# Forming the first network's operand for both groups of heads in one step, with the second group's heads placed pairwise the other way round

## The chip, the core and the metric

The kernel runs on one core of a Trainium2 chip. The metric is device time in microseconds (us) of one execution; lower is better. The time before is the median of three runs.

## What is computed

Landmark attention for 4 batches of 8 heads (576 rows, head size 64, 32 landmarks), followed by two feed-forward networks over the 2304 rows:

```python
q_lm = q.reshape(B, H, m, S // m, D).mean(axis=3)     # 32 landmarks a head
k_lm = k.reshape(B, H, m, S // m, D).mean(axis=3)
A = sm(q, k_lm); Bm = sm(q_lm, k_lm); C = sm(q_lm, k)
Z = Bm.transpose(0, 1, 3, 2) / (norms of Bm)
for _ in range(6):
    Z = 2 * Z - Z @ Bm @ Z
attn = A @ Z @ C @ v
h = attn @ w_in;  x = leaky_relu(h) @ w_out           # first network, 512 -> 2048 -> 512
xn = x / rms(x) * rms_g                               # second network
out = (silu(xn @ w_gate) * (xn @ w_val)) @ w_out2
```

## The kernel before

The kernel never forms the attention's output. For each batch `b` it computes W = Z C v (64 x 32 a head, `wt`) and multiplies it into `w_in` before anything meets A: for each quarter `c` of the 2048 columns, M = W^T w_in, a 32 x 512 block for each head. A and M, each split into a high and a low part of the type fp32r, then feed the first network's hidden layer: h = A M, summed over all heads. M is the "operand of the first network" in the title.

**Heads and groups.** The eight heads are two groups `g` of four (NG = 2). A group's four heads lie side by side in tiles of 128 partitions: the generator `heads` gives for head `h` the 64 input rows it uses (0 to 63 for even `h`, 64 to 127 for odd) and its 32 landmark partitions, `32 * h` to `32 * h + 32`. So a product of a head of 64 input rows and 32 output rows uses a 64x32 part of TensorE's 128x128 array: its rows are given by where the inputs lie, its columns by the output's partitions. In both groups head 0 stands on rows 0 to 63 and columns 0 to 31, head 1 on rows 64 to 127 and columns 32 to 63, head 2 on rows 0 to 63 and columns 64 to 95, head 3 on rows 64 to 127 and columns 96 to 127. Half of the array's eight 64x32 parts are used by one group, and the other group uses the same half.

**Where such sets of four products stand.** `form_m` (line 740): M, 64x32 parts, 512 columns of output, for each of 4 batches, 4 quarters and 2 groups, so 32 sets. `chain` (line 512: landmark scores, 304 columns, two sets for each batch and group; later smaller ones at lines 578, 616, 632, 659) and `soft_a` (line 682: scores of A, 288 columns, two sets for each batch and group). All of these are plain fp32, and the trace shows each such product as two MATMUL instructions, so a set of four products is eight instructions. The large products (lines 773 and 839: the first network; 1120 and 1363: the second) are fp32r, one instruction each, on the whole array.

**Evacuation of M.** A set of `form_m` writes one bank of PSUM (tag `pa`, two banks in all, shared by `chain` and `soft_a`). A copy to the high part follows (ScalarE or VectorE, helper lines 335 and 337), then a subtraction on VectorE for the low part (line 750). Then the bank is free.

**Order.** All instructions are put in order by a planner in the kernel (`Order`). A task is a Python generator that yields the engines it could use with an assumed length, and what it needs: events, or free buffers of a ring, as `("pa", 1)`. The planner picks among the tasks that can run the one with the lowest start and due time; the due time of a task is its deadline less a length from the table `PAR`. The order it finds is the program's; on the chip each engine runs its own list and waits by semaphores.

```python
def form_m(b, c, g):                       # before: one group at a time
    ...
    yield pe4(512), [("pa", 1), f"chain{b},{g}"] + before
    ...
    e = yield act(450) + dve(512), []
    copy(e, hi, pm)
    yield dve(512), []
    nc.vector.tensor_sub(lo, pm, hi.bitcast(F32))      # line 750
    order.free(pm)
```

Of the kernel before, what the change touches and what calls it, by code (L numbers as in the profile page):

```python
# [8 lines left out]
F32 = mybir.dt.float32  # L9
# [21 lines left out]
    "unit": 2400,  # L31
    "chain": [18400, 20600, 27900, 75000],
    "soft": 5000,
    "form": 2600,
    "conv": 600,
    "load": 400,
    "raw": 6600,
# [130 lines left out]
def pe4(n, count=1):  # L168
    return [("pe", int(count * (n / 0.6 + 26)))]
# [35 lines left out]
def landmark_attention_then_two_ffns(  # L205
# [272 lines left out]

    def heads():

        for h in range(4):
            a = 64 * (h % 2)
            yield h, h // 2, slice(a, a + 64), slice(32 * h, 32 * h + 32)

    def chain(b, g):

# [19 lines left out]
        for i in range(2):  # L508
            yield pe4(HB), [(pa, 1)]
            sc = bank(pa)  # L510
            for h, p, rows, lm in heads():
                nc.tensor.matmul(
                    sc[lm, :HB], qsum[rows, p], kt[p][rows, i * HB:(i + 1) * HB],
                    start=True, stop=True,
                )
            on = yield act(HB - 30) + dve(HB), []
            copy(on, e[:, i * HB:(i + 1) * HB], sc[:, :HB])
            order.free(sc)
# [55 lines left out]

        yield pe4(P, 4), [(pa, 1)]
        pr = bank(pa)
        for h, p, rows, lm in heads():
            nc.tensor.matmul(
                pr[lm, :M], bb[lm, 1, :], bb[lm, 1, :], start=True, stop=True
            )  # L580
# [31 lines left out]
        def cv(out, c):  # L612
            vt = v_in[b, g]
            n = P if c < NKC - 1 else KREST
            for h in range(4):
                nc.tensor.matmul(
                    out[32 * h:32 * h + 32, :],
                    et[:n, c * P + 32 * h:c * P + 32 * h + 32],
                    vt[:n, c, 64 * h:64 * h + 64],
                    start=(c == 0), stop=(c == NKC - 1),  # L620
                )

        for k in range(NEWTON):
            last = k == NEWTON - 1
            n0 = 1 if last else 0
            needs = [(pa, 1)]
            if k == 1:
                needs += [f"v{b},{g}", f"turned{b},{g},0", f"turned{b},{g},1"]
            yield pe4((320, 320, 128)[min(k, 2)]), needs
            pr = bank(pa)  # L630
            for h, p, rows, lm in heads():
                nc.tensor.matmul(
                    pr[lm, :2 * M].rearrange("p (a m) -> p a m", m=M)[:, n0:],
                    rz[lm, 0, :], rz[lm, 2 * n0::2, :], start=True, stop=True,
                )
            if k == 0:
                nc.tensor.transpose(pr[:, 2 * P:3 * P], e[:, 3 * P:4 * P], ident)
                nc.tensor.transpose(pr[:KREST, 3 * P:], e[:, 4 * P:S], ident)
            elif k == 1:
                for c in range(NKC):  # L640
                    cv(pr[:, 2 * P:2 * P + 64], c)
                order.free(v_in[b, g])
            yield dve(2 * M), []
            nc.vector.tensor_add(
                rz[:, 2 * n0::2, :],
                pr[:, :2 * M].rearrange("p (a m) -> p a m", m=M)[:, n0:],
                rz[:, 1 + n0:, :],
            )
            if k == 0:
                order.aside(turned(1, pr))  # L650
            elif k == 1:
                order.aside(scaled(pr))
            else:
                order.free(pr)
        yield pe4(64), [(pa, 2), ("wt", 1), f"cv{b},{g}"]
        pw = bank(pa), bank(pa)
        wt = new("wt", wq, [P, 2, M])
        for h, p, rows, lm in heads():
            nc.tensor.matmul(
                pw[p][rows, :M], t1[lm, :], z[lm, :], start=True, stop=True  # L660
            )
# [10 lines left out]
    def soft_a(b, g, h):  # L672

        j = 2 * b + h
        before = [f"soft{j - 1},{i}" for i in range(NG)] if j else []
        before += [f"soft{j},0"] if g else []
        yield pe4(SB), [("pa", 1), ("x2", 1), f"ksum{b},{g}", f"q{b},{g}"] + before
        kt, qt = k_in[b, g], q_in[b, g]
        nb = SB // M
        ps = bank("pa")  # L680
        for _, p, rows, lm in heads():
            nc.tensor.matmul(
                ps[lm, :SB], kt[p][rows, S:], qt[p][rows, h * SB:(h + 1) * SB],
                start=True, stop=True,
            )
        if h == 1:
            order.free(kt[0], qt[0])
        x2 = new("x2", att, [P, 2 * SB])
        order.begun(f"soft{j},{g}")
        yield dve(SB), []  # L690
        xf, xt = x2[:, :SB], x2[:, SB:]
        x = xf.rearrange("p (a m) -> p a m", m=M)
        st = att_tile([P, 2, nb], "st")
        nc.vector.transpose(xf, ps[:, :SB])  # L694
        order.free(ps)
        yield dve(SB), []
        nc.vector.reduce_max(st[:, 0, :], x, axis=AX.X)
        e = yield pool(SB - 60) + dvep(SB), []
        engine[e].tensor_sub(x, x, st[:, 0, :].unsqueeze(2).to_broadcast([P, nb, M]))
        yield act(SB), []  # L700
        nc.scalar.activation(xf, xf, AF.Exp, scale=SCALE / GRP)
        yield dve(SB), []
        nc.vector.reduce_sum(st[:, 0, :], x, axis=AX.X)
        yield dvep(nb), []
        nc.vector.tensor_scalar_add(st[:, 0, :], st[:, 0, :], EPS_SM)
        yield dvep(nb + 30), []
        nc.vector.reciprocal(st[:, 1, :], st[:, 0, :])
        e = yield pool(SB - 60) + dvep(SB), []
        engine[e].tensor_mul(x, x, st[:, 1, :].unsqueeze(2).to_broadcast([P, nb, M]))
        yield dve(SB), []  # L710
        nc.vector.transpose(xt, xf)
        e = yield act(SB) + dve2(SB), [f"at{j}"] if g else [("at_hi", 1)]
        if g == 0:
            at_hi[j], at_lo[j] = part("at_hi", at_all, SB)
            order.begun(f"at{j}")
        copy(e, at_hi[j][:, g, :], xt)
        e = yield pool(SB) + dvep(SB), []
        engine[e].tensor_sub(at_lo[j][:, g, :], xt, at_hi[j][:, g, :].bitcast(F32))
        order.free(x2)
        order.done(f"a{j},{g}")  # L720

    m_order = list(dict.fromkeys((j // 2, f // q4) for _, j, f in units))
    m_left = {(b, g): NC for b in range(B) for g in range(NG)}
    mm_hi, mm_lo = {}, {}

    def form_m(b, c, g):
        first = g == 0
        before = [f"mm{b},{c}"] if g else [("m_hi", 1)]
        i = m_order.index((b, c))
        if first and i:  # L730
            before.append("mm{},{}".format(*m_order[i - 1]))
        before += [f"w_in{c},{2 * g + p}" for p in range(2)]
        yield pe4(512), [("pa", 1), f"chain{b},{g}"] + before
        if first:
            mm_hi[b, c], mm_lo[b, c] = part("m_hi", m_all, 512)
            order.begun(f"mm{b},{c}")
        hi, lo = mm_hi[b, c][:, g, :], mm_lo[b, c][:, g, :]
        pm = bank("pa")
        for h, p, rows, lm in heads():
            nc.tensor.matmul(  # L740
                pm[lm, :], wt_in[b, g][rows, p], w_in_sb[c][rows, 2 * g + p, :].bitcast(F32),
                start=True, stop=True,
            )
        m_left[b, g] -= 1
        if m_left[b, g] == 0:
            order.free(wt_in[b, g])
        e = yield act(450) + dve(512), []
        copy(e, hi, pm)
        yield dve(512), []
        nc.vector.tensor_sub(lo, pm, hi.bitcast(F32))  # L750
        order.free(pm)
        order.done(f"m{b},{c},{g}")
# [682 lines left out]
    with tc.manual_schedule():  # L1435
# [60 lines left out]
        for b in range(B):  # L1496
            when = first(lambda j, f: j == 2 * b)
            for g in range(NG):
                before = PAR["chain"][b] + PAR["load"] - g * 200 + PAR["form"]
                order.add(when, before, load_k(b, g))  # L1500
                order.add(when, before - PAR["q"], load_q(b, g))
                order.add(when, before - PAR["v"][b], load_v(b, g))
                order.add(when, PAR["chain"][b] + PAR["form"], chain(b, g))
                for h in range(2):
                    w = first(lambda j, f: j == 2 * b + h)
                    order.add(w, PAR["soft"] + PAR["last"] * (b == B - 1), soft_a(b, g, h))
                for c in range(NC):
                    w = first(lambda j, f: (j // 2, f // q4) == (b, c))
                    order.add(w, PAR["form"] + PAR["last"] * (b == B - 1), form_m(b, c, g))
        nc.sync.dma_start(g_sb, rms_g)  # L1510
        order.add(due(0), PAR["h"], ffn1_h(0))
        order.add(due(0) + 1500, PAR["y"], ffn1_y(0))
# [90 lines left out]
```

## Time and profile before

| | |
|---|---|
| median of 3 runs | 855.62 us (853.45 to 857.05) |
| profiled execution: its own time, and the span from its first to its last instruction | 853.5 us, 851.4 us |
| busy share of the span: TensorE (PE), VectorE (DVE), ScalarE (ACT), GpSimd (POOL) | 96%, 74%, 40%, 17% |
| mean granted TensorE clock | 0.984 of full speed |
| line 740 (M): instructions, busy time | 256, 33.5 us, between 36.7 and 345.2 us |

The profile is of one execution. PE is matrix multiplication, PEld the loading of weights beside it. A line number is that of the kernel before. A row of a timeline gives start and length in us, engine, line, operation, what is written and read, shape, and the number of instructions that were merged; in brackets the idle time of the engine before it, and what ended it. A merged row's length runs to the end of its last instruction, which lies past the start of the next row because matmuls are pipelined; what a row costs PE is read from its start to the start of the next row.

### The profile page before, as it was taken

What the parts mean: (1) busy time and instruction counts of PE and PEld (TensorE: products, weight loads), DVE (VectorE), ACT (ScalarE), POOL (GpSimd) and SP (SyncE); (2) the same over time, 40 slices, a digit from 0 to 9 for tenths busy, and PEclk for the clock granted to TensorE, in tenths of its full rate; (3) what the DMA queues carried; (4) which work ended last, traced back from release to release, by engine and by line L of the source; (5) the groups of instructions that cost most, each with busy time, mean ns of one, the idle gap of its engine ahead of it and who ended that gap; (6) DMA issues with size and microseconds to landing.
All of it is one profiled execution on the core that took longest, in us unless ns stands there. A gap on an engine that the chain in (4) does not pass through costs nothing. (4 is left out here: it accounts for less than half of the span.)

```text
span 851.4 us, 17835 instructions
## 1 busy us (share of the span) xinstructions
PE 821.6 (96%) x6902; PEld 754.5 (89%) x6902; DVE 631.2 (74%) x1405; ACT 340.8 (40%) x816; POOL 147.2 (17%) x183
## 2 busy tenths in 40 slices
PE   4899999999999999999989999999999999999998
PEld 1388789988888887999979999999999999999998
DVE  6699885556465866778679877777777659998991
ACT  4677474444344544545444343333333222222220
POOL 2241231002040531210032131211222000000000
PEclk9599999999999999999999999999999999999999
DMA  9874773453723703546421243222321399653601
GB/s 326 315 252 138 246 258 121 167 181 113 247 79 111 252 30 107 163 161 195 167 85 56 68 131 106 106 105 106 106 92 57 118 349 356 188 169 111 182 31 50
DMA packets 80549, 131.97 MB, mean 155 GB/s; under 512 B 6224, under 2 KB 50256, under 8 KB 79568
## 3 DMA queue, kind: packets, MB, share of 16 engines
q1 hardware_dynamic: 80464, 130.84, 46.0%
q8 instruction: 54, 0.88, 0.4%
q14 instruction: 31, 0.25, 0.1%
HBM read 87.95 MB, written 42.86 MB: 154 GB/s over the span
## 5 line engine op out<-in xcount | busy, mean ns | idle before, releaser
L839 PE MATMUL py<-g_hi,w 128*128 128x288 f32 x1024 | 210.7, 299 | 0.0
L839 PEld LDWEIGHTS py<-g_hi,w 128*128 128x128 f32 x1024 | 163.5, 188 | 12.0 <-issue 11.2
L839 PE MATMUL py<-g_lo,w 128*128 128x288 f32 x512 | 150.7, 294 | 0.0
L773 PE MATMUL ph<-at,mm 128*128 128x288 f32 x768 | 127.5, 305 | 1.5 <-ACT hs L792 1.4
L773 PEld LDWEIGHTS ph<-at,mm 128*128 128x128 f32 x768 | 109.5, 191 | 16.7 <-ACT hs L792 6.0
L789 ACT ACTIVATE g_hi<-ph 128x288 fp32r<-128x288 f32 x128 | 52.5, 410 | 127.1 <-PE ph L773 114.0
L839 PEld LDWEIGHTS py<-g_lo,w 128*128 128x128 f32 x512 | 96.3, 188 | 0.0
L795 DVE TENSOR_TENSOR g_lo<-hs,g_hi 128x288 fp32r<-128x288 f32 x104 | 49.2, 473 | 55.3 <-ACT hs L792 54.8
L792 ACT ACTIVATE hs<-ph 128x288 f32<-128x288 f32 x128 | 52.1, 407 | 0.0
L1214 ACT ACTIVATE cc<-cc 128x288 f32<-128x288 f32 x48 | 21.4, 445 | 68.4 <-DVE cc L1211 68.2
L1185 ACT ACTIVATE hs<-ph 128x288 f32<-128x288 f32 x48 | 19.6, 408 | 62.3 <-PE ph L1120 62.3
L1120 PE MATMUL py<-w,wt 128*128 128x288 f32 x288 | 43.2, 298 | 0.0
L1120 PE MATMUL py<-w,mm 128*128 128x288 f32 x288 | 42.6, 296 | 0.3 <-DVE g_lo L1178 0.3
L373 ACT ACTIVATE raw<-raw 128x512 f32<-128x512 f32 x52 | 35.2, 680 | 16.5 <-DMA raw<-w_val 10.2
L335 ACT COPY hs<-ph 128x288 f32<-128x288 f32 (+1 forms) x49 | 18.8, 384 | 57.0 <-PE ph L1363 33.0
L1120 PEld LDWEIGHTS py<-w,wt 128*128 128x128 f32 x288 | 39.9, 189 | 0.5 <-DVE g_lo L1181 0.2
L1120 PEld LDWEIGHTS py<-w,mm 128*128 128x128 f32 x288 | 39.6, 188 | 0.8 <-DVE g_lo L1178 0.5
L1188 DVE TENSOR_TENSOR cc<-g_hi,py 128x288 f32<-128x288 f32 x48 | 21.6, 450 | 23.8 <-PE py L1120 23.8
L740 PE MATMUL pa<-w_in,wt 64*32 64x512 f32 x256 | 33.5, 626 | 2.3 <-DVE x L694 1.3
L795 POOL TENSOR_TENSOR g_lo<-hs,g_hi 128x288 fp32r<-128x288 f32 x24 | 20.9, 872 | 66.7 <-ACT hs L792 64.5
L1196 DVE TENSOR_TENSOR us<-cc,g_lo 128x288 f32<-128x288 f32 x46 | 22.9, 498 | 12.2 <-ACT cc L1214 12.2
L1196 DVE TENSOR_TENSOR us<-hs,cc 128x288 f32<-128x288 f32 x45 | 26.9, 599 | 5.6 <-DMA u_dram<-us 1.7
(302 smaller groups left out, 1743.1 us busy)
## 6 DMA issues: line engine op xcount, KB each, us to landing
u_dram<-us SPq DMA_DIRECT2D x48, 288.0 KB, 2.1
wo_dram<-ct SPq DMA_DIRECT2D x42, 256.0 KB, 2.3
raw<-w_out SPq DMA_DIRECT2D x20, 512.0 KB, 4.3
y_dram<-ys SPq DMA_DIRECT2D x60, 144.0 KB, 2.2
yin<-y_dram SPq DMA_DIRECT2D x14, 576.0 KB, 4.8
yin<-u_dram SPq DMA_DIRECT2D x20, 384.0 KB, 6.2
raw<-w_gate SPq DMA_DIRECT2D x12, 512.0 KB, 3.7
raw<-w_val SPq DMA_DIRECT2D x12, 512.0 KB, 4.8
```

The source lines that it names most:

```text
L373: nc.scalar.activation(high.bitcast(F32), high.bitcast(F32), AF.Prelu, scale=2.0 ** -112, alpha=2.0 ** 32)
L740: nc.tensor.matmul(pm[lm, :], wt_in[b, g][rows, p], w_in_sb[c][rows, 2 * g + p, :].bitcast(F32), start=True, stop=True,)
L773: nc.tensor.matmul(ph[:, :SB], w[b, c][:, g, o:o + P], x[j][:, g, :], start=(n == 0), stop=(n == 3 * NG - 1),)
L789: nc.scalar.activation(g_hi[u], ph[:, :SB], AF.Prelu, alpha=0.01)
L792: nc.scalar.activation(hs, ph[:, :SB], AF.Prelu, alpha=0.01)
L795: engine[e].tensor_sub(g_lo[u], hs, g_hi[u].bitcast(F32))
L839: nc.tensor.matmul(yacc[i][d][:, :SB], w[f][:, d * P:(d + 1) * P], x[u], start=(f == f0 and n == 0), stop=(f == f1 - 1 and n == 2),)
L1120: nc.tensor.matmul(pp[:, :SB], w[f][:, i, c * P:(c + 1) * P], x[b][1][:, k, c, :], start=(first and n == 0), stop=(n == 5), skip_group_che ...
L1185: nc.scalar.activation(sg, pp["a"][:, :SB], AF.Silu)
L1188: nc.vector.tensor_add(f32("c21", "cc"), t["u2"], pp["c"][:, :SB])
L1196: engine[e].tensor_mul(us[0][:, h, :], sg, t[name])
L1214: nc.scalar.activation(t["c12"], t["c12"], AF.Silu)
```

## The change

`form_m` is one task for both groups: it asks for two banks of `pa`, for the chains of both groups and for all four pieces of `w_in`, issues the eight products of the two groups one behind the other, and then starts two tasks `split_m`, one for each group, that evacuate as before. In `heads`, the landmark partitions of head `h` of group 1 become those of head `h ^ 1`: heads 0 and 1 change places, and heads 2 and 3. With that, the second group stands on the other four 64x32 parts of the array. All users of `heads` take the group, so that the landmark partitions agree everywhere. In the table, the length `form` goes from 2600 to 4500, which moves the deadlines of the loads, the chain and `form_m` that are worked out from it. Behind line 740 the same code stands nine lines further down in the changed kernel, before it some five (740 is 743, 750 is 759, 773 is 782, 839 is 848, 512 is 517, 682 is 687).

```diff
-    "form": 2600,
+    "form": 4500,
...
-    def heads():
+    def heads(g):
         for h in range(4):
             a = 64 * (h % 2)
-            yield h, h // 2, slice(a, a + 64), slice(32 * h, 32 * h + 32)
+            m = 32 * (h ^ g)
+            yield h, h // 2, slice(a, a + 64), slice(m, m + 32)
...
-            for h in range(4):
+            for h, _, _, lm in heads(g):
                 nc.tensor.matmul(
-                    out[32 * h:32 * h + 32, :],
-                    et[:n, c * P + 32 * h:c * P + 32 * h + 32],
+                    out[lm, :],
+                    et[:n, c * P + lm.start:c * P + lm.stop],
...
-    def form_m(b, c, g):
-        first = g == 0
-        before = [f"mm{b},{c}"] if g else [("m_hi", 1)]
+    def form_m(b, c):
         i = m_order.index((b, c))
-        if first and i:
+        before = [("m_hi", 1)] + [f"chain{b},{g}" for g in range(NG)]
+        if i:
             before.append("mm{},{}".format(*m_order[i - 1]))
-        before += [f"w_in{c},{2 * g + p}" for p in range(2)]
-        yield pe4(512), [("pa", 1), f"chain{b},{g}"] + before
...
+        before += [f"w_in{c},{k}" for k in range(2 * NG)]
+        yield pe4(512), [("pa", NG)] + before
+        mm_hi[b, c], mm_lo[b, c] = part("m_hi", m_all, 512)
+        order.begun(f"mm{b},{c}")
+        pm = [bank("pa") for _ in range(NG)]
+        for g in range(NG):
+            for h, p, rows, lm in heads(g):
+                nc.tensor.matmul(
+                    pm[g][lm, :], wt_in[b, g][rows, p],
+                    w_in_sb[c][rows, 2 * g + p, :].bitcast(F32), start=True, stop=True,
+                )
...
+        for g in range(NG):
+            order.aside(split_m(b, c, g, pm[g]))
+
+    def split_m(b, c, g, pm):
         hi, lo = mm_hi[b, c][:, g, :], mm_lo[b, c][:, g, :]
...
         e = yield act(450) + dve(512), []
         copy(e, hi, pm)
         yield dve(512), []
         nc.vector.tensor_sub(lo, pm, hi.bitcast(F32))
...
-                for c in range(NC):
-                    w = first(lambda j, f: (j // 2, f // q4) == (b, c))
-                    order.add(w, PAR["form"] + PAR["last"] * (b == B - 1), form_m(b, c, g))
+            for c in range(NC):
+                w = first(lambda j, f: (j // 2, f // q4) == (b, c))
+                order.add(w, PAR["form"] + PAR["last"] * (b == B - 1), form_m(b, c))
```

The number of products is unchanged, and so is the number of MATMUL instructions on PE. The order changes in many places, since the planner plans anew. Three of them, by the order of the programs' instructions on an engine (a row is a line and its operation, what is written and read, and a count of equal instructions; here a count is of products):

PE, the second quarter of batch 0, before, where the two groups of M stand apart (this is the first of them):

```order
L773 MATMUL ph<-at,mm 128x288 x12
L740 MATMUL pa<-w_in_115,wt 32x512 x4
L773 MATMUL ph<-at,mm 128x288 x6
L839 MATMUL py<-g_hi,w_117 128x288 x2
L839 MATMUL py<-g_lo,w_117 128x288
```

The same quarter in the changed kernel:

```order
L848 MATMUL py<-g_hi,w_117 128x288 x2
L848 MATMUL py<-g_lo,w_117 128x288
L743 MATMUL pa<-w_in_115,wt 32x512 x8
L848 MATMUL py<-g_hi,w_117 128x288 x2
L848 MATMUL py<-g_lo,w_117 128x288
```

The two sets of four have become one run of eight, and output products of the first network stand on both sides of it.

PE, the first two quarters of batch 1, before:

```order
L839 MATMUL py<-g_hi,w_117 128x288 x2
L839 MATMUL py<-g_lo,w_117 128x288
L740 MATMUL pa<-w_in_115,wt 32x512 x12
L773 MATMUL ph<-at,mm 128x288 x12
L740 MATMUL pa<-w_in_115,wt 32x512 x4
L773 MATMUL ph<-at,mm 128x288 x6
```

And changed, where a set of `soft_a` (L687, it needs a bank of `pa`) stands directly behind the first run of eight:

```order
L848 MATMUL py<-g_hi,w_117 128x288 x2
L848 MATMUL py<-g_lo,w_117 128x288
L743 MATMUL pa<-w_in_115,wt 32x512 x8
L687 MATMUL pa<-qt_533,kt_512 32x288 x2
L687 MATMUL pa<-qt_534,kt_513 32x288 x2
L782 MATMUL ph<-at,mm 128x288 x12
L743 MATMUL pa<-w_in_115,wt 32x512 x8
L782 MATMUL ph<-at,mm 128x288 x6
```

Twelve products in a row, then four more, have become two runs of eight with `soft_a` and two hidden units between them.

DVE, the evacuation at the same place in the changed kernel (`mm` is M, `ys` an output of the first network's sums; L699 frees the bank of `soft_a`):

```order
L871 TENSOR_TENSOR ys<-ys,py 128x288 x2
L337 CAST mm<-pa 128x512
L871 TENSOR_TENSOR ys<-ys,py 128x288
L759 TENSOR_TENSOR mm<-pa,mm 128x512 x2
L871 TENSOR_TENSOR ys<-ys,py 128x288
L699 STREAM_TRANSPOSE x_1458<-pa 128x288
L415 SCALAR_TENSOR_TENSOR w_in_116<-raw 128x512
```

One high part is now copied by DVE and both low parts follow on DVE; the other high part is copied by ACT. Over the kernel 17 of the 32 high parts are copied by ACT and 15 by DVE (before 29 and 3).

## Rows read from the trace of the kernel before

**Rows 1.** The page, parts 1 and 2: PE's share, and its clock in 40 slices.

```profile
PE 821.6 (96%) x6902; PEld 754.5 (89%) x6902; DVE 631.2 (74%) x1405; ACT 340.8 (40%) x816; POOL 147.2 (17%) x183
...
PEclk9599999999999999999999999999999999999999
```

**Rows 2.** Busy time of each engine by stretch of the span.

```profile
36.60:45.00 8.40, 8.18 (x31) 4.42 (x32) 6.18 (x15) 6.13 (x13) 1.96 (x3) 0.50 0.99 362
45.00:100.00 55.00, 53.61 (x573) 43.63 (x571) 49.56 (x131) 33.75 (x84) 17.75 (x21) 0.99 0.66 206
100.00:200.00 100.00, 99.82 (x764) 88.84 (x768) 61.64 (x133) 51.21 (x129) 15.59 (x20) 1.00 0.58 191
```

**Rows 3.** What PE waited for: us in total, times, longest us.

```profile
PE py L632 <- DVE rz L587: 2.0, 1, 2.0
PE pa L740 <- DVE mm L750: 1.0, 1, 1.0
```

**Rows 4.** Groups by line and form: count, busy us, mean ns of one, idle before.

```profile
L740 PE MATMUL pa<-w_in,wt 64*32 64x512 f32 x256 | 33.5, 626 | 2.3 <-DVE x L694 1.3 <-DVE mm L750 1.0
...
L750 DVE TENSOR_TENSOR mm<-pa,mm 128x512 fp32r<-128x512 f32 x32 | 21.8, 688 | 11.7 <-ACT mm L335 11.5
...
L335 ACT CAST mm<-pa 128x512 fp32r<-128x512 f32 x29 | 17.0, 586 | 15.7 <-PE pa L740 15.6
...
L1039 PE MATMUL pa<-cc,ones 96*128 96x288 f32 x16 | 5.4, 417 | 3.0 <-DVE cc L1034 3.0
```

**Rows 5.** Timeline of PE: one set of line 740 alone, and the next row.

```profile
54.75 1.06 PE L740 MATMUL pa<-w_in,wt 64*32 64x512 f32 x8
55.74 1.05 PE L773 MATMUL ph<-at,mm 128*128 128x288 f32 x6
```

**Rows 6.** Timeline of PE: two sets of line 740 in a row, and the next row.

```profile
343.31 1.92 PE L740 MATMUL pa<-w_in,wt 64*32 64x512 f32 x16
345.17 1.06 PE L773 MATMUL ph<-at,mm 128*128 128x288 f32 x6
```

**Rows 7.** Timeline of PE: the two instructions of one product of line 1039.

```profile
452.38 0.65 PE L1039 MATMUL pa<-cc,ones 96*128 96x288 f32 x2
```

**Rows 8.** Timeline of all engines around the first M, at half clock.

```profile
36.66 3.64 PE L740 MATMUL pa<-w_in,wt 64*32 64x512 f32 x16 [1.31 <-DVE x L694]
...
40.36 0.58 ACT L335 CAST mm<-pa 128x512 fp32r<-128x512 f32 x1 [0.54 <-PE pa L740]
...
41.00 5.00 PE L773 MATMUL ph<-at,mm 128*128 128x288 f32 x17 [0.16 <-ACT mm L335]
```

**Rows 9.** Timeline of PE: sets of lines 512 and 682, each with the row behind it.

```profile
61.88 1.23 PE L512 MATMUL pa<-kt,qsum 64*32 64x304 f32 x16
63.03 1.05 PE L773 MATMUL ph<-at,mm 128*128 128x288 f32 x6
...
114.49 1.17 PE L682 MATMUL pa<-qt,kt 64*32 64x288 f32 x16
115.59 0.54 PE L839 MATMUL py<-g_hi,w 128*128 128x288 f32 x2
```

**Rows 10.** Timeline of all engines around the first M of batch 1.

```profile
98.38 0.69 DVE L337 CAST mm<-pa 128x512 fp32r<-128x512 f32 x1
```

**Rows 11.** Timeline of PE: line 616, and the next row.

```profile
80.88 0.90 PE L616 MATMUL pa<-vt,big 128*32 128x64 f32 x40
81.71 0.31 PE L632 MATMUL pa<-rz 32*32 32x64 f32 x8
```

**Rows 12.** Timeline of PE at the start, at half clock.

```profile
5.91 1.17 PE L682 MATMUL pa<-qt,kt 64*32 64x288 f32 x4 [5.91 <-DMA qt<-qT]
7.40 0.69 PE L682 MATMUL pa<-qt,kt 64*32 64x288 f32 x2 [0.32 <-DMA qt<-qT]
7.53 0.72 PE L512 MATMUL py<-kt,qsum 64*32 64x304 f32 x2
7.85 0.72 PE L682 MATMUL pa<-qt,kt 64*32 64x288 f32 x2
```

More of the change, by code (lines that the diff above doesn't have):

```diff
@@ L510, in chain @@
             sc = bank(pa)
-            for h, p, rows, lm in heads():
+            for h, p, rows, lm in heads(g):
                 nc.tensor.matmul(
@@ L576, in chain @@
         pr = bank(pa)
-        for h, p, rows, lm in heads():
+        for h, p, rows, lm in heads(g):
             nc.tensor.matmul(
@@ L630, in chain @@
             pr = bank(pa)
-            for h, p, rows, lm in heads():
+            for h, p, rows, lm in heads(g):
                 nc.tensor.matmul(
@@ L657, in chain @@
         wt = new("wt", wq, [P, 2, M])
-        for h, p, rows, lm in heads():
+        for h, p, rows, lm in heads(g):
             nc.tensor.matmul(
@@ L680, in soft_a @@
         ps = bank("pa")
-        for _, p, rows, lm in heads():
+        for _, p, rows, lm in heads(g):
             nc.tensor.matmul(
@@ L722, in landmark_attention_then_two_ffns @@
     m_order = list(dict.fromkeys((j // 2, f // q4) for _, j, f in units))
-    m_left = {(b, g): NC for b in range(B) for g in range(NG)}
+    m_left = {b: NC for b in range(B)}
     mm_hi, mm_lo = {}, {}
-    def form_m(b, c, g):
-        first = g == 0
-        before = [f"mm{b},{c}"] if g else [("m_hi", 1)]
+    def form_m(b, c):
         i = m_order.index((b, c))
-        if first and i:
+        before = [("m_hi", 1)] + [f"chain{b},{g}" for g in range(NG)]
+        if i:
             before.append("mm{},{}".format(*m_order[i - 1]))
-        before += [f"w_in{c},{2 * g + p}" for p in range(2)]
-        yield pe4(512), [("pa", 1), f"chain{b},{g}"] + before
-        if first:
-            mm_hi[b, c], mm_lo[b, c] = part("m_hi", m_all, 512)
-            order.begun(f"mm{b},{c}")
-        hi, lo = mm_hi[b, c][:, g, :], mm_lo[b, c][:, g, :]
[L738 to L746, printed above, removed]
+        before += [f"w_in{c},{k}" for k in range(2 * NG)]
[4 more added lines that the diff above has]
+        for g in range(NG):
+            for h, p, rows, lm in heads(g):
+                nc.tensor.matmul(
+                    pm[g][lm, :], wt_in[b, g][rows, p],
+                    w_in_sb[c][rows, 2 * g + p, :].bitcast(F32), start=True, stop=True,
+                )
+        m_left[b] -= 1
+        if m_left[b] == 0:
+            for g in range(NG):
+                order.free(wt_in[b, g])
+        for g in range(NG):
+            order.aside(split_m(b, c, g, pm[g]))
+    def split_m(b, c, g, pm):
+        hi, lo = mm_hi[b, c][:, g, :], mm_lo[b, c][:, g, :]
         e = yield act(450) + dve(512), []
```

## The prediction, made before the changed kernel was run

> **What bounds the kernel now.** I read the page first. PE is busy 96% of the span, and from the third of the 40 slices on its clock stands at nine tenths or more in every slice [rows 1]. Then the table by stretch: in the part that the change touches, up to 345 us, PE is busy 53.6 of 55 us and then 99.8 of 100, while DVE, the next engine, has 49.6 of 55 and then 61.6 of 100 [rows 2]. The list of PE's waits is short: apart from the start, the only one at line 740 that has to do with its own banks is 1.0 us, once [rows 3]. So nearly every microsecond that PE doesn't need ends the program earlier, unless a new wait takes its place. That makes two questions: how much PE time do eight products at a time save, and how much of it is lost to waits?
>
> **What a set of four costs now.** Line 740 has 256 instructions [rows 4], that is 128 products, or 32 sets of four. A set that stands alone takes PE 0.99 us, from 54.75 to 55.74 [rows 5]. Two in a row take 1.86 us, 343.31 to 345.17 [rows 6]. The second set adds 0.87, and 0.12 is what entering and leaving the set costs. What would the eight instructions cost one after another? A product on the whole array, line 1039, shows it: its two instructions of 288 columns end 0.65 us after the start [rows 7], one lasts 0.417 [rows 4], so the second begins about 0.23 behind the first, 0.81 ns a column. Eight instructions of 512 columns would take 8 x 512 x 0.81 = 3.3 us in single file, and 1.7 two abreast. They take 0.87: four are abreast, and a set costs its two instructions, 2 x 512 x 0.81 = 0.83.
>
> **What eight abreast would cost.** The second group's four products then lie on the other four parts, so by the array's plan all eight can run at once, and a pair of sets costs what one costs now, 0.99, and a little for starting eight instead of four; I take 0.04, an estimate that is a third of the 0.12 of enter and leave. So 1.03 a pair.
>
> The timeline has line 740 in eleven runs of two sets (one of them inside a run of three, at 97.25), and ten sets alone. The first run of two is at half clock: 3.64 us on its row, which like other rows is 0.07 longer than the time to the next start, so 3.57 [rows 8]. Before: 10 x 1.86 + 10 x 0.99 + 3.57 = 32.1. After, 16 runs: 15 x 1.03 + 3.57 / 2 + 0.07 = 15.5 + 1.9 = 17.3. **Saved: 14.8 us.**
>
> **What the exchange of places gives elsewhere.** Sets of lines 512 and 682 of the two groups that stand next to each other now also lie on different parts. A pair takes 1.15 and 1.10 now [rows 9]; abreast it would take half of that, plus half of enter and leave and the starts, about 0.66. In the changed order I count three such pairs of line 512 (687 and 517 in the new numbering stand next to each other too, at the last batch, which I leave out) and four of 682: 7 x 0.46 = 3.2, less 0.2 for two sets that stood together and now stand apart. **Saved: 3 us**, between 0 (if nothing runs abreast) and 3.5. The smaller sets of the chain keep their parts and cost the same.
>
> **What the change adds.** No instruction is added on PE. The waits are the open part.
>
> First M of batch 0: it is formed at half clock, and what follows needs it at once: line 773 ran on at 41.00, when ACT had finished the second high part, 40.36 + 0.58 [rows 8]. With eight abreast both banks are full together, and DVE has three passes of 0.69 in series behind them (one copy, two subtractions [rows 4, 10]), 2.1 us, where it had one left behind the second set. So of the 1.7 us saved there I give back 1.
>
> Banks: a run of eight takes both banks of `pa`, and the first comes free after a copy and a subtraction, 0.69 + 0.69 = 1.4 us at the soonest, the second after 2.1. Fifteen of the 16 runs have only lines 773 and 839 of the old numbering behind them for 0.9 us or more, which use other banks; a wait there can come only from needing M itself. At one place, the first run of batch 1, line 687 stands directly behind, with an addition for `ys` among DVE's passes: some 1.8 us of wait. There stood the 1.0 us wait before [rows 3], so 0.8 more.
>
> DVE: twelve copies move from ACT (0.586 each) to DVE (0.69), 8.3 us over the 300 us in which M is formed. Between 100 and 200 us DVE has 38 us to spare and PE doesn't feel it; between 45 and 100 it has 5.4 [rows 2], and there a late VectorE result reaches PE. I put 1 us on that, and 1 us on the first batch's chains, which are planned in another order; the nearest row is the 2.0 us for which PE waits there once already [rows 3].
>
> Together 1 + 0.8 + 1 + 1, **about 4 us lost**. The bounds: 1 us, if DVE's slack takes all but the first M; 9 us, if in addition every second run costs the 1.0 us of [rows 3].
>
> **The sum.** 14.8 + 3 - 4 = 13.8 us. The profiled execution took 853.5 us, 2.1 more than its span; it would become 839.7. The median of the runs is 855.6, 2.1 above the profiled one, so I say 841.5 for the median.
>
> **Rival 1: two products on the same columns don't run side by side.** In the new placing head 0 of the first group and head 1 of the second write the same 32 partitions, into two banks, from different rows of the array. No long set of before does that: in a set of line 740 each product has columns of its own. If they take turns, a pair costs two turns as now, 1.86; all that is left is ten times the 0.12 of enter and leave, less waits of 2 to 4: 856 us, no change. For eight abreast speaks that the columns can all be fed at once at full length: line 616 has four streams over all 128 rows, the same input as eight streams over 64, and its 40 instructions of 64 columns take 0.83 us [rows 11], where single file would be 40 x 64 x 0.81 = 2.1 and four abreast 0.52 plus enter and leave.
>
> The Trainium skill has a rule that speaks for this rival: TensorEngine Tiling (Array Packing), section Gotcha 1: PSUM Pressure, says that different row tiles write to different banks and can't access one bank at the same time. Taken strictly, the two row halves of each bank would take turns, a set of four would cost 1.7 us, and the pair after the change no less than before. The set of [rows 5] has products on both row halves into one bank and takes 0.99, so this trace does not agree; whether the rule holds in the changed kernel's pattern no run here shows.
>
> **Rival 2: the second group starts one turn late.** Each product is two instructions one behind the other, and the second must wait for the first on its own part. If PE looked ahead over four products only, the second group would begin with the first one's second turn: three turns, 3 x 0.43 + 0.12 = 1.4 a pair instead of 1.03. Then 16 x 0.4 = 6 us of the gain are missing and half of the 3: 849 us. Against it: at the start four instructions of line 682, then two more, then two of line 512 begin at 7.53, and only at 7.85 the last two of line 682 [rows 12], though the program issues all eight of line 682 first. So a product can start over waiting ones.
>
> By the Trainium skill, TensorE: Matmul & The Clock Gate, section Part 3: Packing small matmuls, The mechanism, matmuls start and end in program order. Strictly so, each second instruction would hold up the next product's first, and four abreast as in [rows 5] could not be; [rows 12] don't agree with it either.
>
> **Rival 3, slower: the banks become the bound.** All 16 runs ask for two banks and both groups' chains at once, and hold both. If behind or ahead of every run PE waits for a copy and a subtraction, 1.4 us, this is 22 us against 17.8 saved: 860 us. It decides from 1.1 us a run on. For it: `pa` has two banks for three users, and DVE is at 90% between 45 and 100 us [rows 2]. Against it: eleven runs of two sets needed both banks before too, and that cost 1.0 us once [rows 3]; and most runs have large products behind them.
>
> **Chances.** The forecast 0.70, with a range of its own of 836 to 848 (1 to 9 us lost, and 2 us by which medians differ). Rival 1 0.11, rival 2 0.10, rival 3 0.09. The range that holds eight in ten takes in rival 2 and the forecast's bounds: 836 to 852. Half a per cent, 4.3 us, is about what a measurement of this kernel can tell from no change. Faster than 851.3: the forecast and most of rival 2, 0.78. Slower than 859.9: most of rival 3 and a little of rival 1, 0.08. Between them 0.14.
>
> **What would show it.** Right: line 743 has 256 instructions in 16 runs, each about 1.03 us to the next row's start at full clock, and some 17 to 18 us busy in all instead of 33.5; line 517's pairs take 0.65 at batch 1; the last instruction of line 782 comes 12 to 15 us earlier than that of line 773 before, and the second network takes as long as before. Rival 1 shows as runs of 1.86, rival 2 as runs of 1.4, rival 3 as a list of waits in which line 743, 687 or 782 waits for DVE or ACT for over 10 us more. Wrong in its cause would be a gain that comes from other stretches than those up to 345 us, or a lower clock.

## The result, and the profile after

The changed kernel takes **844.8 us** (median of four executions, 842.93 to 846.54); the kernel before, beside it on the same chip, 855.06 us. The ratio is **0.9883, with a 95% interval of 0.9863 to 0.9903**: 1.2% faster. The forecast was 841.5 us, its range 836 to 852. The profiled execution took 843.61 us with a span of 841.4, so it gained 9.9 us on the one of before.

The page of the changed kernel, parts 1 and 2, for [rows 1]:

```profile
PE 806.3 (96%) x6902; PEld 748.9 (89%) x6902; DVE 629.3 (75%) x1406; ACT 334.3 (40%) x802; POOL 157.7 (19%) x196
...
PEclk9699999999999999999999999999999999999999
```

PE is busy for 15.3 us less, with the same number of instructions, and still for 96% of a shorter span. The groups of M's products and of the copies on DVE, by form, for [rows 4]:

```profile
L743 PE MATMUL pa<-w_in,wt 64*32 64x512 f32 x256 | 19.2, 629 | 1.1 <-DVE x L699 1.1
...
L337 DVE CAST mm<-pa 128x512 fp32r<-128x512 f32 x15 | 10.3, 689 | 6.2 <-PE pa L743 6.1
```

33.5 us of M have become 19.2. One run of eight on the timeline of PE, with the row behind it, for [rows 5, 6]:

```profile
57.04 1.09 PE L743 MATMUL pa<-w_in,wt 64*32 64x512 f32 x16
58.06 0.40 PE L848 MATMUL py<-g_hi,w 128*128 128x288 f32 x1
```

From its start to the next row's it takes 1.02 us, where two sets took 1.86 and one set 0.99. All 14 runs at full clock that another row follows at once take 1.02 (the first of batch 1 has a wait of 1.84 us behind it, and the very first is at half clock). So eight products run side by side; e1 below tests it. The neighbours do too, where both banks are free: the pair of line 687 of batch 2, for [rows 9]:

```profile
227.66 0.72 PE L687 MATMUL pa<-qt,kt 64*32 64x288 f32 x16
228.31 0.53 PE L848 MATMUL py<-g_hi,w 128*128 128x288 f32 x2
```

0.65 us instead of 1.10; this holds for three pairs of line 687 and one of line 517 (0.67 at 193.66). Not so at batch 1: its two pairs of line 517, at 61.43 and 63.64, take 0.91 and 1.42, since the second set of each starts late for its bank.

Where do the 10 us come from? The table by stretch, cut at the start of the last instruction of lines 773 and 782 (the last hidden units of the first network); the columns are length, then busy time of PE, PEld, DVE, ACT and POOL, PE's clock, the DMA's share and its GB/s. Before:

```profile
0.00:427.63 427.63, 408.02 (x3699) 344.36 (x3700) 297.67 (x775) 217.57 (x558) 91.76 (x125) 0.97 0.54 182
427.63:851.40 423.77, 413.53 (x3205) 410.15 (x3203) 333.49 (x631) 123.28 (x258) 55.44 (x58) 1.00 0.39 128
```

And after:

```profile
0.00:419.38 419.38, 392.40 (x3700) 338.71 (x3700) 297.44 (x774) 210.67 (x545) 103.53 (x138) 0.98 0.56 183
419.38:841.40 422.02, 413.93 (x3205) 410.15 (x3203) 331.91 (x633) 123.61 (x258) 54.22 (x58) 1.00 0.39 131
```

In the first stretch PE works 408.02 - 392.40 = 15.6 us less. Its idle time, length less busy time, goes from 19.6 to 27.0: 7.4 us come back as waits. 15.6 - 7.4 leaves 8.2 us. Another 1.75 us come behind it, where nothing was changed.

The clock alone doesn't make the 15.6 us. At the start it stood at half for longer before than in this profile; length, busy time of PE and the clock (third from the end) of one stretch, before and after:

```profile
18.70:46.00 27.30, 21.78 (x259) 0.50 0.88 330
...
18.70:46.00 27.30, 19.78 (x274) 0.69 0.91 336
```

But e8, a second profile of the same changed kernel with 0.53 there, has 392.67 us of busy time up to its last hidden unit, almost the same.

The list of PE's waits after, for [rows 3]:

```profile
PE py L637 <- DVE rz L592: 3.7, 1, 3.7
PE ph L782 <- ACT hs L801: 3.4, 4, 1.5
...
PE pa L687 <- DVE mm L759: 1.8, 1, 1.8
PE pa L1048 <- DVE cc L1043: 1.8, 2, 1.4
...
PE ph L782 <- DVE mm L759: 1.1, 2, 0.9
...
PE pa L1017 <- POOL misc L1012: 0.4, 1, 0.4
```

Two lines of the same list before:

```profile
PE ph L773 <- ACT hs L792: 1.4, 3, 0.7
...
PE pa L1008 <- DVE misc L1003: 1.2, 1, 1.2
```

The first of after stands in batch 0's chain (2.0 before), the second at hidden units behind `soft_a` and the output copies on ACT (1.4 before). The fourth and the last are the seam to the second network: the longest of the two waits of line 1048 and the one of line 1017 are 1.8 us together, where lines 1039 and 1008 waited 3.0 and 1.2.

### The profile page after: what moved, and what is told of

Its sections match the earlier page's. It is cut to its first block, busy times and chain, and to the rows that moved or that the text cites. A ratio compares the mean times of both kernels' runs of the same rounds, so it can differ in the third digit from the quotient of the medians.

```text
span 841.4 us, 17833 instructions
## 1 busy us (share of the span) xinstructions
PE 806.3 (96%) x6902; PEld 748.9 (89%) x6902; DVE 629.3 (75%) x1406; ACT 334.3 (40%) x802; POOL 157.7 (19%) x196
## 4 chain that ended last, share of the span: by engine, by line
PE 81%; DVE 9%; DMA 4%; ACT 3%; issue 2%; SPq 0%; POOL 0%; ACTq 0%; DVEq 0%; POOLq 0%
PE py L848 19%; PE py L1129 17%; PE ph L782 10%; PE py L1372 9%; PE ph L1129 8%; PE ph L1372 5%; PE pa L1129 4%; PE pa L1372 2%; PE pa L743 2%; DMA raw<-w_out 1%; PE pa L637 1%; PE pa L687 1%; DMA u_dram<-us 1%; DMA kt<-kT 1%; PE pa L621 1%
## 5 line engine op out<-in xcount | busy, mean ns | idle before, releaser
L804 DVE TENSOR_TENSOR g_lo<-hs,g_hi 128x288 fp32r<-128x288 f32 x99 | 46.7, 472 | 54.6 <-ACT hs L801 53.2
L804 POOL TENSOR_TENSOR g_lo<-hs,g_hi 128x288 fp32r<-128x288 f32 x29 | 24.1, 832 | 118.1 <-ACT hs L801 111.5
L1197 DVE TENSOR_TENSOR cc<-g_hi,py 128x288 f32<-128x288 f32 x48 | 21.6, 451 | 25.6 <-PE py L1129 25.3
L1372 PE MATMUL py<-w,w 128*128 128x256 f32 x216 | 26.8, 281 | 0.0
```

Source lines behind the costliest of these rows:

```text
L804: engine[e].tensor_sub(g_lo[u], hs, g_hi[u].bitcast(F32))
L1197: nc.vector.tensor_add(f32("c21", "cc"), t["u2"], pp["c"][:, :SB])
L1372: nc.tensor.matmul(pp[name][:, :HM], x[:, p, :], o_home[r][:, p, i, :], start=(tag is not None and m == 0), stop=(m == 3 * NP2 - 1), skip_ ...
```

## The experiments

There are twelve experiments, four at a time on one chip (e1 to e4, e5 to e8, e9 to e12); the kernel before ran beside each four and took 854.22, 854.5 and 854.15 us. "Idle" is PE's idle time up to the last hidden unit, from the table by stretch of each profile: 27.0 in the first profile of the changed kernel, 19.6 before. The 31.5 us that the expectations name are another count, the sum of PE's idle times by group over the whole execution (26.3 before).

| kernel | median us | ratio to before (95%) | idle |
|---|---|---|---|
| e1: changed kernel, same parts | 855.51 | 1.0017 (1.0003 to 1.0031) | 23.5 |
| e2: before, exchange alone | 849.75 | 0.9953 (0.9938 to 0.9968) | 24.4 |
| e3: form 2600 | 846.82 | 0.9911 (0.9884 to 0.9938) | 25.5 |
| e4: copies on ACT | 844.77 | 0.9895 (0.9866 to 0.9924) | 26.0 |
| e5: form 3000 | 843.38 | 0.9871 (0.9849 to 0.9893) | 20.2 |
| e6, e11: form 6500 | 841.56, 839.54 | 0.9851 (0.9824 to 0.9878), 0.9822 (0.9803 to 0.9841) | 23.4, 22.3 |
| e7: evacuation first | 847.18 | 0.9912 (0.9884 to 0.9941) | 25.5 |
| e8, e12: changed kernel again | 843.81, 843.84 | 0.9877 (0.9848 to 0.9907), 0.9868 (0.9851 to 0.9884) | 24.8, 25.3 |
| e9: before, form 4500 | 857.54 | 1.0036 (1.0024 to 1.0049) | 21.7 |
| e10: form 6500, same parts | 853.74 | 0.9988 (0.9973 to 1.0004) | 21.8 |

**Is it the exchange of places? e1 and e2.** e1 takes the exchange back and keeps everything else, the order too:

```diff
-            m = 32 * (h ^ g)
+            m = 32 * h
```

> The changed kernel with the exchange of places taken back (both groups on the same four parts of the array), the order of all instructions the same. If the gain comes from eight products running abreast: a run of line 743 takes 1.86 us to the next row's start instead of 1.02 at the 15 places at full clock (12.6 us more), the neighbouring sets of lines 517 and 687 some 0.46 us more at six places (2.8 us), a few us of this hidden in waits that are there anyway: 855 to 859 us, no faster than the kernel before. Rival, the gain comes from the new order and the joint task: runs of 1.02 or a time that stays at 843 to 847 us.

It took 855.51 us: the gain is gone. The group of its products, and the table by stretch up to its last hidden unit:

```profile
L743 PE MATMUL pa<-w_in,wt 64*32 64x512 f32 x256 | 32.5, 624 | 1.0 <-DVE x L699 1.0
```

```profile
0.00:430.26 430.26, 406.74 (x3699) 342.89 (x3700) 298.03 (x774) 210.96 (x545) 102.62 (x138) 0.97 0.54 179
```

Its runs take 1.85 us. So forming both groups in one task is worth nothing by itself. And the idle time is 430.26 - 406.74 = 23.5 us already here: of the 7.4 us of new waits, 3.9 come with the new order, not with faster products, if one profile of each may be compared (e8 and e12 give an idea of the chance in it). The list of waits shows where they stand:

```profile
PE py L637 <- DVE rz L592: 3.3, 1, 3.3
...
PE ph L782 <- ACT hs L801: 2.3, 4, 1.4
...
PE ph L782 <- DVE mm L759: 1.1, 2, 0.9
...
PE pa L687 <- DVE mm L759: 1.0, 1, 1.0
```

Three of the four are there without the exchange: the first and the third nearly as long as in the changed kernel, the second 2.3 instead of 3.4 (2.2 in e8). The wait of line 687 behind the first run of batch 1 grows from 1.0 to 1.8, because the products end 0.83 us sooner and the evacuation doesn't: line 687 starts 2.93 us after the run's start here and 2.92 in the changed kernel.

e2 is the counterpart, the exchange in the kernel before and in its order:

```diff
-    def heads():
+    def heads(g):
...
-            yield h, h // 2, slice(a, a + 64), slice(32 * h, 32 * h + 32)
+            m = 32 * (h ^ g)
+            yield h, h // 2, slice(a, a + 64), slice(m, m + 32)
```

> The kernel before with the exchange of places alone: each group's M is still a task of its own, the order of instructions is that of the kernel before. If parts of the array are what counts, the sets of different groups that stand next to each other there run abreast without the joint task: eight runs of line 741 at 1.02 instead of 1.86 (6.7 us), four of line 513 and four of line 683 at 0.65 instead of 1.1 (3.7 us), and no new wait for banks: 10 us faster than before, 844 to 846 us, as fast as the whole change. Rival, the joint task is needed for it: 852 to 856 us, since in neighbouring sets that are separate tasks the second starts only when its own bank is free.

849.75 us lies between the two expectations. Two rows of its PE timeline, each with the next, tell a part of why (line 741 is 740 of before):

```profile
328.25 1.92 PE L741 MATMUL pa<-w_in,wt 64*32 64x512 f32 x16
330.10 0.53 PE L840 MATMUL py<-g_hi,w 128*128 128x288 f32 x2
...
340.46 1.09 PE L741 MATMUL pa<-w_in,wt 64*32 64x512 f32 x16
341.48 0.80 PE L774 MATMUL ph<-at,mm 128*128 128x288 f32 x4
```

Two sets of different groups take 1.02 us; two sets of one group, which stand on the same parts (two quarters of the second group here), take 1.85, in one kernel and one table of places. Six pairs ran at 1.02, where the expectation counted eight, two of one group at 1.85, and nine sets stood alone; a pair at 331.88 took 1.26, its second set starting late, and the first run and the run of three at batch 1 are left out here. The waits rose too, though the order is that of before: idle 424.59 - 400.17 = 24.4 us. The one behind the first sets of batch 1, 1.0 us in [rows 3], became 1.84, and the clock fell after it:

```profile
99.87 1.75 PE L741 MATMUL pa<-w_in,wt 64*32 64x512 f32 x8 [1.84 <-DVE mm L751]
101.55 1.81 PE L774 MATMUL ph<-at,mm 128*128 128x288 f32 x6
```

This set of four took 1.68 us instead of 0.99. In the changed kernel the clock did not fall behind the wait of the same length.

**Are the waits the planner's order? e3, e5, e6, e9.** Each changes one number of the table, in the changed kernel (4500) or, e9, in the kernel before (2600):

```diff
-    "form": 4500,
+    "form": 2600,
```

> The changed kernel with the table's length form back at 2600, so that the deadlines are those of before and the planner makes another order. The products keep their 14 us if these come from the array alone (runs of 1.02). The waits are then the planner's luck: 841 to 849 us. Rival, the longer length is what makes room for both banks: PE's idle time grows by over 4 us from 31.5 and the time is 849 us or more.

e5 has 3000 there, e6 6500:

> The changed kernel planned anew with the length form 3000 in place of 4500; products, places and evacuation are the same. Theory A, the new waits of 5 us hang on the order that the planner happens to find: line 743 keeps 1.02 us a run and 18.2 us in all, PE's idle time moves by 2 us or more from the 31.5 us of the changed kernel, and the time moves with it, anywhere from 839 to 848. Theory B, the waits belong to the first batches' chains, which no order shortens: idle time within 1.5 us of 31.5 and 843.5 to 846.

> As the run before with the length form 6500, so that runs of M are planned earlier. Theory A: idle time again elsewhere, 839 to 848; its sign is not said beforehand, but the two lengths and 4500 and 2600 differ among themselves by more than 3 us. Theory B: 843.5 to 846. If one of the two stands under the changed kernel with an interval that does not hold 1, the waits behind the change were partly avoidable by order alone.

Line 743 kept its time (17.6 to 18.2 us from start to start), idle moved between 20.2 and 25.5 us, and the medians between 841.6 and 846.8: theory A held, theory B fell. Of the idle times only e5's is far outside what the changed kernel's own three profiles show (24.8 to 27.0), and the interval of e6 overlaps that of e8, so its lead is not shown before e11. And idle time alone doesn't rank them. e5 has the least and is only 0.4 us faster than e8, the changed kernel on the same chip: PE is busy 396.3 us in its first network instead of e8's 392.7, and its second network takes 2.1 us longer. Its table by stretch shows one place where time goes, behind a wait of 1.5 us at 219:

```profile
220.00:224.00 4.00, 4.00 (x26) 3.66 (x26) 0.70 (x4) 0.10 (x1) 0.00 (x0) 0.57 0.32 115
224.00:228.00 4.00, 4.00 (x42) 3.37 (x42) 2.20 (x6) 2.05 (x6) 0.00 (x0) 1.00 0.47 145
```

With the clock at 0.57, 4 us hold 26 instructions instead of 42; e8 has no such stretch there. The rest of the 3.6 us was not traced. e9:

> The kernel before with the length form 4500 alone: one group at a time, no exchange. Theory A (the table's number only finds another order): line 740 keeps its 32 to 33 us, and the time is 852 to 860, with no lasting gain. Rival: part of the change's 10 us comes from earlier planning of M, and this kernel is faster than before by 2 us or more, 850 to 853.

857.54 us, 0.4% slower than before: the number gives nothing by itself.

**Are the copies on DVE the loss? e4.** The planner plans as before, but every high part is copied by ACT:

```diff
-        e = yield act(450) + dve(512), []
+        yield act(450) + dve(512), []
+        e = "act"
```

> The changed kernel, planned as it is, but every high part of M is copied by ACT (the 15 copies that the plan gives to DVE are written for ACT). DVE does 10.3 us less, ACT 8.8 us more; the two high parts of a run now follow each other on ACT. If the new waits come from DVE holding the banks with three passes in series, the wait behind the first run of batch 1 falls from 1.8 to about 1.2 us and PE's idle time from 31.5 by 1 to 3 us: 841 to 844 us. Rival, the waits come from the planner's order and not from DVE: idle time and the time within 1 us of the changed kernel's, 843 to 846 us.

844.77 us, as the changed kernel: taking the copies from DVE gains nothing on balance. At the first run of batch 1 it is worse: ACT stands in front of its copies waiting for a piece of `w_in`, and PE's wait there grows from 1.84 to 2.98. So up to some 1 us gained elsewhere could be hidden. The timeline of all engines of e4:

```profile
96.27 1.09 PE L743 MATMUL pa<-w_in,wt 64*32 64x512 f32 x16
...
98.41 0.68 ACT L373 ACTIVATE raw<-raw 128x512 f32<-128x512 f32 x1 [3.54 <-DMA raw<-w_in]
98.97 1.06 ACT L335 CAST mm<-pa 128x512 fp32r<-128x512 f32 x2
...
100.33 0.69 PE L687 MATMUL pa<-qt,kt 64*32 64x288 f32 x8 [2.98 <-DVE mm L760]
```

**Evacuation first: e7, with e8 beside it.** e7 plans M's evacuation as if it were due 20 us earlier:

```diff
             order.aside(split_m(b, c, g, pm[g]))
+            order.branches[-1][0] -= 20000
```

> The changed kernel, with the two tasks that evacuate M put 20 us earlier in due time, so that the planner places copies and subtractions of M ahead of other work that is ready. Theory C, the added waits come from banks of pa that are given back late: the 1.84 us wait of line 687 behind the first run of batch 1 falls to about 1.4 (two passes of 0.69), PE's idle time falls by 1 us or more, and the time is 842 to 844. Theory A: the wait behind that run may fall, but idle time as a whole moves by the luck of a new order, 842 to 849.

> The changed kernel itself once more, on the chip of the three others, as their yardstick: 844 to 846, and a ratio to the kernel before of 0.987 to 0.990. Its trace tells how much PE's idle time (31.5 us) and single waits differ between two executions of one program: under 1 us is expected.

Theory C fell: the wait of line 687 is 1.84 us still, a second one of that kind appears, idle is 25.5, and 847.18 us is 3 more than e8's 843.81, though the two intervals overlap. In its profile the seam's wait is 3.0 us again, and some 7 us at half clock follow it (last section). e8's ratio is the one expected (its time 0.2 us less), and it gives a measure of chance: its idle is 2.2 us under that of the first profile of the same program, more than the 1 us that I expected.

**A faster version: e6 again as e11, with e10 and e12.** e10 is e6 with the edit of e1.

> Form 6500 with eight products in a run, but both groups on the same four parts; the order of all instructions is that of form 6500. Theory A: what the exchange is worth does not hang on the order: runs of M take 1.86 instead of 1.02, 13.4 us in 16 runs, 1.5 more at line 687, and 3 of it lie in waits that are there anyway, so 850 to 854, some 11 us over form 6500. Rival: form 6500 is good by itself, and this kernel stands under 848.

> Form 6500 once more, beside the changed kernel on the same chip. If its lead was real: 840.5 to 842.5, 2 to 3 us under the changed kernel, and a ratio to before of 0.983 to 0.987. If it was luck: 843 to 845.

> The changed kernel again as the yardstick of these four: 843.5 to 845.5, ratio 0.986 to 0.990.

e11 took 839.54 us, 1 us less than expected, and e12 843.84, and the intervals of their ratios don't overlap: form 6500 beats the changed kernel by 4.3 us here and by 2.3 in e6 against e8, and before by 1.5 to 1.8%. e10, in the order of e11 and with runs of 1.85 us, took 853.74: there the exchange is worth 12 to 14 us (against e6 by the ratios, against e11), some 11 between e1 and the changed kernel. One thing that differs in form 6500 is the first M. The changed kernel's timeline of PE and DVE there, for [rows 8]:

```profile
36.55 2.90 PE L743 MATMUL pa<-w_in,wt 64*32 64x512 f32 x16 [1.14 <-DVE x L699]
36.99 0.47 DVE L699 STREAM_TRANSPOSE x<-pa 128x288 f32<-128x288 f32 x1
...
40.14 1.29 DVE L759 TENSOR_TENSOR mm<-pa,mm 128x512 fp32r<-128x512 f32 x2 [0.89 <-ACT mm L335]
...
41.48 0.79 PE L782 MATMUL ph<-at,mm 128*128 128x288 f32 x4 [0.93 <-DVE mm L759]
```

And e11's:

```profile
33.48 0.47 DVE L699 STREAM_TRANSPOSE x<-pa 128x288 f32<-128x288 f32 x1
...
35.65 2.33 PE L743 MATMUL pa<-w_in,wt 64*32 64x512 f32 x16
...
38.29 5.65 PE L782 MATMUL ph<-at,mm 128*128 128x288 f32 x18 [0.30 <-ACT mm L335]
```

In the changed kernel `soft_a` holds both banks of `pa` up to the first M. The first group's products wait 1.14 us, and the second group's start 0.97 us after the first's, when the transposition at 36.99 has freed the second bank: the two groups run side by side for about half of their time only. In e11 the transposition was over at 33.95, all eight products have started within 0.42 us, and hidden units run on at 38.29 instead of 41.48, 3.2 us earlier.

In these two profiles the lead doesn't come from that start. Eighteen hidden and twelve output instructions later, at the same point of the order, the next row stands at the same time, in the changed kernel and in e11:

```profile
45.82 0.95 PE L782 MATMUL ph<-at,mm 128*128 128x288 f32 x6
...
45.92 0.95 PE L782 MATMUL ph<-at,mm 128*128 128x288 f32 x6
```

The clock took the 3.2 us back: between 40 and 46 us it stood at 0.58 in e11 and at 1.00 in the changed kernel, and e11's first 18 hidden instructions took 5.45 us, up to the next row at 43.74. And e5 has the early start too:

```profile
37.72 5.69 PE L782 MATMUL ph<-at,mm 128*128 128x288 f32 x18 [0.28 <-ACT mm L335]
```

It takes 843.38 us all the same. By the last hidden unit e11 leads by 3.7 to 6.1 us (413.76 against 417.5 to 419.8). A part is read off its rows: its two pairs of line 517 at batch 1 take 0.67 each, and PE's wait for line 759 in front of line 687 at batch 1 is 0.39 instead of 1.84, since output products of the first network stand between it and the run of eight. The rest was not traced, and no experiment takes these places apart.

## Why the prediction was right

The time came in the range and for the reason given: eight products run side by side, and a part of the saving comes back as waits. No rival came. But the sizes behind M's products are off, and the signs named beforehand did not all come: the pairs of line 517 at batch 1 took 0.91 and 1.42 us instead of 0.65, the last hidden unit came 8 to 10 us earlier instead of 12 to 15, and the second network didn't take as long as before. (The sum itself is 0.3 us off: 855.62 - 13.8 is 841.8, not 841.5.) Term by term:

| term | predicted | measured |
|---|---|---|
| M's products | -14.8 | -14.0: 15 runs of 1.02, and the first of 2.83, 18.1 instead of 32.1 |
| neighbours, lines 517 and 687 | -3 | -1.8: three pairs of 687 at 0.65 and one of 517 at 0.67; two of 517 held up by a bank |
| waits of the first network | +4 (1 to 9) | +7.4 in this profile, +5.2 and +5.7 in e8 and e12 |
| last hidden unit | 12 to 15 earlier | 8.2 earlier (10.1 and 7.8 in e8 and e12) |
| second network | as before | 1.75 shorter (1.2 and 1.9 in e8 and e12) |
| sum of the profile | -13.8 | -10.0 |

**Eight abreast.** A run takes 1.02 us for 1.03 predicted; what starting eight instead of four costs was put at 0.04, and is 0.03. Rival 1 (1.86 a run) and rival 2 (1.4) are refuted by all 14 runs at full clock. The Trainium skill's rule in TensorEngine Tiling (Array Packing), section Gotcha 1: PSUM Pressure, that different row tiles can't access one bank at the same time, doesn't hold here either: a run of eight writes each of its two banks from both row halves, in 1.02 us.

**The first M** was mis-sized. I took half of 3.57 us for its products and gave 1 us back for the evacuation, 0.7 gained. From the first product to the hidden units that run on it took 41.00 - 36.66 = 4.34 us before and takes 41.48 - 36.55 = 4.93 now (4.93 in e8 and e12 too), 0.6 lost. I had counted the banks that M holds, but not that it needs two free ones at its start. The row was there: in [rows 8] the first M waits 1.31 us for line 694, the transposition that frees a bank of `soft_a`; I had read only the 1.0 us in [rows 3] as a wait for banks. The Trainium skill, Trainium Kernel Development and Optimization, section Best Practices, says that tiling TensorE speeds up compute but not the evacuation of PSUM; this stretch agrees: the products take 2.83 us instead of 3.57, and the way to the hidden units is 0.6 longer.

**The banks.** The wait of line 687 at batch 1 was forecast at 1.8 us, from the passes of DVE behind the run, and is 1.84. It is the only one of its kind and size. Rival 3 asked for 1.1 us a run; the other runs have large products behind them, as argued.

**The waits as a whole** are the term that was too small, within its bounds. e1 splits them, as far as single profiles go: 3.9 us of the 7.4 come with the order that the planner found, before anything is faster; e3, e5 and e6 show that another number finds another order, with 20 to 26 us of idle time. The rest is 3.5, 1.3 and 1.8 us in the three profiles of one program, so some 2 us of it are chance. What stands in all three is the wait of line 687 behind the first run of batch 1, 0.8 more than in e1; that PE comes earlier to work that DVE and ACT finish no earlier is shown there, and argued for the rest. e2 has 4.8 us more than before in the order of before. I had put 1 us on DVE's twelve copies; e4 shows no such gain without them.

**The second network** gained 1.75 us that I didn't foresee: the two waits at its seam were 4.2 us and are 1.8. They are 2.0 in e1's and e4's lists too, and 4.2 in those of e6, e7 and e11, so they go with the order. That hid a part of the missing gain: luck, not forecast.

## What to carry to other kernels

Small products that stand one behind the other can cost hardly more than one set of them if they lie on parts of the array that the others leave free (here 1.02 us for two sets and 0.99 for one); look at which rows and columns each uses, and change places where two groups use the same half. When work on the bottleneck gets shorter, the other engines' times stay, so take a part of the saving off for waits (here a third to a half), and ask of a larger step not only how long it holds its buffers but whether all of them are free when it starts. Where a planner sets the order, try its numbers again after the change: here that was worth another 2 to 4 us.

## What the runs showed of the hardware that was not expected

A wait of PE can cost more than its length. At the seam PE waits twice, at line 1048 and some ten us later at line 1017 (1039 and 1008 before). In eight of the fourteen profiles the granted clock fell to half (the 1.2 GHz level) at one of the two: in e2, e3, e6, e7, e10 and e11 at the first, a wait of 2.6 to 3.0 us, in e9 and e5 behind the second, 1.4 and 2.0 us. It stayed there for 3.4 us, in e7 for 6.8. The length of the wait alone doesn't decide it. Behind the first wait of before and of e9, 3.0 us, the clock did not fall, nor behind the 1.4 to 1.6 us of the changed kernel's three profiles, e1 and e4; behind e9's second wait, 1.4 us, it did. Its row on PE's timeline, and the stretch of the table in which it was at half:

```profile
449.80 0.64 PE L1008 MATMUL pa<-ones,misc 128*96 128x1 f32 x6 [1.40 <-DVE misc L1003]
...
451.80:455.20 3.40, 3.40 (x16) 3.40 (x15) 2.01 (x4) 0.41 (x1) 1.17 (x1) 0.50 0.23 87
```

The table by stretch of e7, where it lasted longest; the first numbers are length and busy time of PE, and the clock is the third from the end:

```profile
424.00:426.00 2.00, 0.40 (x4) 0.17 (x2) 2.00 (x1) 0.00 (x0) 2.00 (x2) 1.00 0.00 0
426.00:428.00 2.00, 0.64 (x1) 0.50 (x2) 1.90 (x6) 0.00 (x0) 0.42 (x1) 0.65 0.00 0
428.00:430.00 2.00, 2.00 (x9) 1.85 (x8) 1.61 (x4) 0.00 (x0) 0.00 (x0) 0.50 0.00 0
...
432.00:434.00 2.00, 2.00 (x12) 2.00 (x11) 1.44 (x4) 0.28 (x1) 0.00 (x0) 0.64 0.00 0
434.00:436.00 2.00, 2.00 (x17) 2.00 (x16) 1.92 (x5) 1.08 (x1) 0.00 (x0) 1.00 0.63 251
```

9 instructions in 2 us, and 17 once the clock is back. PE is busy for 6.0 us of the 6.8 at half clock, so some 3 us are lost behind a wait of 3.0, an estimate from these numbers. One program differs in it from execution to execution: after the last batch's wait near 302 us (1.5 to 2.1 us) the clock fell in the first and third profile of the changed kernel and not in the second, whose span was the shortest. What decides it is open.
